# Remainder tiles behind the kv products, and two kv products in one: a fused attention and MLP kernel on one core

## The chip, the core and the metric

The kernel runs on one core of a Trainium2 chip. A core has a matrix engine (PE, with its weight loader PEld), a vector engine (DVE), a scalar engine (ACT), GpSimd (POOL) and a queue engine (SP); each works through its own instructions in order and waits for the others by semaphores. Transfers are issued from SP, ACT or POOL and are carried out by 16 DMA engines. The metric is the device time of one execution in microseconds (us). The kernel before was timed six times: median 290.68 us, from 290.37 to 290.84.

## The reference

Eight batches of eight heads, 576 positions, head size 64. For each batch and head, `kv = kᵀ v` (64x64), `out = q kv`, and `out` is divided by its root mean square over the head's 64 elements and multiplied by `g_norm`. The heads side by side make rows `x` of 512. Then comes an MLP with a layer norm ahead of it and a residual:

```python
xn = (x - mean(x)) / sqrt(var(x) + 1e-6) * g_ln
out = x + relu(xn @ w_ch1) @ w_ch2        # 512 -> 2048 -> 512
```

Inputs and output are float32; the kernel multiplies in bfloat16.

## The kernel before, in words

**Tiles.** A batch has 576 rows: four *main tiles* of 128 rows and 64 rows left over. The leftovers of two batches (0 and 1, 2 and 3, and so on) make one *remainder tile* (`rem_tile`, named by the odd batch: 1, 3, 5, 7); the four remainder tiles form a ninth block that goes through the MLP last. A text such as "tile (3,2)" means main tile 2 of batch 3.

**Stages of a batch.** POOL loads k, v and q with a cast to bfloat16 (`load`, L92 to L94: two transfers per tensor). `kv_of` (L239) makes kv of all heads with 40 small matmuls, each with a 128x64 piece of k as weights; two heads stand side by side in the two column halves of the PE array, and two ACT copies put the result into `kv_pack`. `turn_q_dma` (L201) copies q on DVE into another order (L203), and SP transposes it by DMA (L205) into `qts[b]`. A tile (`Tile`, L258) then runs `o` (q times kv on PE: four matmuls for a main tile; eight for a remainder tile, which writes the two batches' 64 rows from the two column halves of the array, as `kv_of` does), `sq` (square, ACT), `red` (sum over the head, DVE), `root` (ACT), `y`, `x`, `xc` (three passes on DVE, L303, L322, L332), `var` (ACT) and `turn` (a DMA transpose of 128x512 on SP, L352, or in the first batches four PE transposes) into `xT_blk`, from which the MLP reads. The two PSUM buffers of `o` are freed by `y`.

**MLP.** `mm1` (L403) multiplies a block's `xT_blk` with w1, with ACT's Relu into `m1`; `mm2` (L450) multiplies `m1` with w2 and ends each tile with `finish` (L432): one DVE pass (L434) and two stores issued on SP (L447, L448).

**Order.** Everything is emitted by hand, in slots. `mm1` and `mm2` call `tick()` once for each unit of work (mostly four matmuls of 512 columns), and `tick` first emits what `at(slot, fn)` put into the agenda for that slot, sorted by the slot's fraction. Block b has `mm1` in slots 32b to 32b+15 and `mm2` in 32b+16 to 32b+31; batch 2's `mm1` runs in two halves of two tiles each (slots 64 to 71 and 72 to 79). So a step of the agenda lands on PE between two units of an earlier block's MLP, and on DVE, ACT, SP and POOL at the matching place of their queues. `plan_tile(s, make, turn_at, on_pe)` (L371) puts `o`, `sq`, `red` at s, `y`, `x`, `xc` at s+2, `var` at s+6 and the turn at `turn_at`. The loop at L633 plans the loads, `kv_of`, `turn_q_dma` and tiles of batches 3 to 7, and the remainder tiles 3, 5 and 7; L630 plans remainder tile 1.

**Loads.** `load_batch` (L96) first makes POOL copy one element of a transposed tile to a one-element buffer `gate`: POOL's queue waits there until that transpose has landed, and the batch's six transfers stand behind. Batch b uses buffers b % 2. For batch 4 a second such copy reads the last element of batch 2's block, which is tile (2,3)'s turned rows.

Of the kernel before, what the change touches and what calls it, by code (L numbers as in the profile page):

```python
# [14 lines left out]
def kernel(  # L15
# [11 lines left out]
    nc = tc.nc  # L27
    f32 = mybir.dt.float32
# [5 lines left out]
    B, H, S, D = q.shape  # L34
# [3 lines left out]
    nK = Dm // 128  # L38
    nDe = Dh // 128
    HP = H // 2  # L40
# [3 lines left out]
    J, JJ, JP = 4, 5, 9  # L44
    S_LO = 64 * JJ
    EPS = 1e-6
    NB = 2
# [8 lines left out]
    ps_m = ctx.enter_context(tc.psum_pool(name="ps_m", bufs=1))  # L56
# [15 lines left out]
    q_in = [consts.tile([128, H, JJ, D], bf16, name=f"q_in{i}") for i in range(NB)]  # L72
    k_in = [consts.tile([128, H, JJ, D], bf16, name=f"k_in{i}") for i in range(NB)]
    v_in = [consts.tile([128, H, JJ, D], bf16, name=f"v_in{i}") for i in range(NB)]
    kv_g = consts.tile([128, HP, 128], bf16)
    kv_pack = [consts.tile([128, HP, 128], bf16, name=f"kv_pack{i}") for i in range(4)]
# [9 lines left out]
    def lo(t, b, h0=0, h1=H):  # L86
        return t[b, h0:h1, :S_LO, :].rearrange("h (p j) d -> p h j d", j=JJ)

    def up(t, b, h0=0, h1=H):
        return t[b, h0:h1, S_LO:, :].rearrange("h (p j) d -> p h j d", j=J)  # L90

    def load(dst, t, b, h0=0, h1=H):  # L92
        nc.gpsimd.dma_start(dst[:64, h0:h1], lo(t, b, h0, h1))
        nc.gpsimd.dma_start(dst[64:, h0:h1, :J], up(t, b, h0, h1))  # L94

    def load_batch(b, *after):  # L96
        for element in after:
            nc.gpsimd.tensor_copy(gate, element)  # L98
        load(k_in[b % NB], k, b)
        load(v_in[b % NB], v, b)  # L100
        load(q_in[b % NB], q, b)

    def load_w1(c):
        n = Dh // 4
# [60 lines left out]
    qts, held, blks, rstds, m1s, q_ps = {}, {}, {}, {}, {}, {}  # L165
# [35 lines left out]
    def turn_q_dma(b):  # L201
        q_p = kv_in.tile([128, JJ, H, D], bf16, tag="qp", bufs=2)
        nc.vector.tensor_copy(q_p.rearrange("p j h d -> p h j d"), q_in[b % NB])  # L203
        q_t = qt_pool.tile([128, JJ, HP, 128], bf16, tag="qt", name="qt")
        nc.sync.dma_start_transpose(  # L205
            q_t.rearrange("p j hp t -> p (j hp) t"), q_p.rearrange("p j h d -> p (j h d)"))
        qts[b] = q_t
# [28 lines left out]
            nc.vector.tensor_mul(kv_g[D:, self.hps, D:], self.odd[D:], g[D:])  # L236
            del self.even, self.odd

    def kv_of(b):  # L239
        kv_ps = ps_m.tile([128, HP, D], f32, tag="misc", name="kv_ps")  # L240
        kvp = held[b] = kv_pack[b % 4]
        for hp in range(HP):
            for j in range(JJ):
                for hh in range(2):
                    h = 2 * hp + hh
                    nc.tensor.matmul(kv_ps[hh * D:hh * D + D, hp, :],  # L246
                                     lhsT=k_in[b % NB][:, h, j, :], rhs=v_in[b % NB][:, h, j, :],
                                     start=(j == 0), stop=(j == JJ - 1))
        nc.scalar.copy(kvp[:D, :, :D], kv_ps[:D])  # L249
        nc.scalar.copy(kvp[D:, :, D:], kv_ps[D:])  # L250

    def new_block(n, bufs):
        x_blk = xpool.tile([128, 4, Dm], f32, tag=f"x{n}", bufs=bufs, name="x_blk")
        st_blk = xpool.tile([128, 3, 4], f32, tag=f"st{n}", bufs=bufs, name="st_blk")
        xT_blk = xpool.tile([128, nK, 512], bf16, tag=f"xT{n}", bufs=bufs, name="xT_blk")
        return x_blk, st_blk, xT_blk
# [98 lines left out]
    def main_tile(b, j, pool=None, tag="ops"):  # L355
        q_t, kvp = qts[b], held[b]
        if b not in blks:
            blks[b] = new_block("main", 3)
        return Tile([(slice(0, 128), lambda hp: q_t[:, j, hp, :], kvp)], blks[b], j, pool, tag)

    def rem_tile(b):
        mms = []
        for half, bb in enumerate((b - 1, b)):
            qt, kp = qts.pop(bb), held.pop(bb)
            mms.append((slice(half * 64, (half + 1) * 64),
                        lambda hp, qt=qt: qt[:, J, hp, :64], kp))
        if "rem" not in blks:
            blks["rem"] = new_block("rem", 1)
        return Tile(mms, blks["rem"], b // 2)

    def plan_tile(s, make, turn_at, on_pe):  # L371
        box = []

        def first():
            t = make()
            box.append(t)
            t.o()
            t.sq()
            t.red()

        def second():
            t = box[0]
            t.y()
            t.x()
            t.xc()

        def third():
            box[0].var()

        def fourth():  # L390
            box[0].turn(on_pe)

        at(s, first)
        at(s + 2, second)
        at(s + 6, third)
        at(turn_at, fourth)

    def m1_of(b):
# [20 lines left out]
    def rstd_of(b):  # L419
        rstd = work.tile([128, 4], f32, tag="rstd", bufs=3, name="rstd")  # L420
        nc.scalar.activation(rstd, blks[b][1][:, 2, :], func=AF.Sqrt, scale=1.0 / Dm, bias=eps_sb)  # L421
        nc.vector.reciprocal(rstd, rstd)  # L422
        rstds[b] = rstd
# [45 lines left out]
    def at(slot, fn):  # L469
        agenda.setdefault(int(slot), []).append((slot, fn))  # L470
# [119 lines left out]
    def next_loads():  # L590
        nc.gpsimd.memset(k_in[0][64:, :, J], 0.0)
        nc.gpsimd.memset(v_in[0][64:, :, J], 0.0)
        load_batch(2)

    at(1, before_1)
    at(2, before_2)
    at(5, lambda: t[2].turn(True))
    at(5.1, before_5)
    at(9.5, next_loads)
    at(11, lambda: t[3].turn(True))  # L600
    for i in range(4):
# [17 lines left out]
    at(14.5, q_start)  # L619
    at(19, q_turns)  # L620
    at(22, lambda: kv_of(1))
    for j, s, tn in ((0, 24, 30), (1, 27, 34), (2, 31, 38), (3, 35, 42)):
        plan_tile(s, lambda j=j: main_tile(1, j), tn, True)
    at(46, lambda: rstd_of(1))

    at(36, lambda: kv_of(2))
    at(36.9, lambda: turn_q_dma(2))
    for j, s, tn in ((0, 45, 51), (1, 49, 55), (2, 53, 61), (3, 57.5, 64)):
        plan_tile(s, lambda j=j: main_tile(2, j), tn, False)
    plan_tile(62, lambda: rem_tile(1), 69, False)  # L630
    at(78, lambda: rstd_of(2))

    for b in range(3, B):  # L633
        s = 32 * b
        at(47 if b == 3 else s - 60,
           lambda b=b: load_batch(b, qts[b - 1][:1, J, HP - 1, 127:],
                                  *([blks[2][2][:1, nK - 1, 511:]] if b == 4 else [])))
        d = -41 if b == 3 else -45
        at(s + d + (1 if b < 5 else 0), lambda b=b: kv_of(b))
        at(s + d + 1.7, lambda b=b: turn_q_dma(b))  # L640
        for j in range(J):
            o = s + d + (11 if b == 3 else 13) + 5 * j
            plan_tile(o, lambda b=b, j=j: main_tile(b, j), o + 6, False)
        if b % 2:
            plan_tile(s - 14, lambda b=b: rem_tile(b), s - 8, False)
        at(s + 14, lambda b=b: rstd_of(b))
    at(32 * B + 14, lambda: rstd_of("rem"))


# [56 lines left out]
```

## Time and profile before

| | |
|---|---|
| median of six runs | 290.68 us |
| the profiled execution's own time | 290.74 us |
| its span in the profile | 288.9 us |
| PE busy | 281.9 us, 98% of the span |
| ACT, DVE, POOL busy | 153.3, 149.9, 40.9 us |
| bytes moved | 36.76 MB, mean 127 GB/s |

The span runs from the first to the last instruction; the execution's own time has 1.8 us more around it. PE's ends are modelled and its matmuls overlap, so its busy share hides gaps of some tenths of a microsecond: the starts of neighbouring groups of matmuls are what can be relied on. In the timeline a row is a group of equal instructions, with its start, its length, the engine (SPq is SP's queue, with the issue time of a transfer), the line, the operation, and in brackets the idle time before it with what ended it. Times are from the span's start.

### The profile page before, as it was taken

How to read it: one execution, taken by the hardware profiler on the slowest of the kernel's cores; microseconds unless marked ns; L12 is line 12 of the kernel's file. 1: busy time of each engine (PE TensorE's matmuls, PEld its weight loads, DVE VectorE, ACT ScalarE, POOL GpSimd, SP SyncE). 2: the span in 40 equal slices, each digit the busy share in tenths (PEclk: the TensorE clock that was granted, in tenths of full speed). 3: DMA queues.
4: the chain of work that ended last, by engine and by line, in shares of the span. 5: the costliest groups of instructions: out<-in, count | busy, mean ns of one | idle time of the engine just before them, and what ended most of it. 6: DMA issues, size and time to landing. Idle time of an engine off the chain costs nothing.

```text
span 288.9 us, 5753 instructions
## 1 busy us (share of the span) xinstructions
PE 281.9 (98%) x2295; PEld 158.1 (55%) x2295; DVE 149.9 (52%) x331; ACT 153.3 (53%) x333; POOL 40.9 (14%) x69
## 2 busy tenths in 40 slices
PE   8999999999999999999999999999999999999994
PEld 3579746995479644444444444444444444444444
DVE  5774119838897783764376935762578200220022
ACT  3577844985379733872288318921893066016400
POOL 8522510050005004100500032000000000000000
PEclk9999999999999999999999999999999999999999
DMA  7999999979886959996994189947203410230033
GB/s 217 198 208 203 198 189 197 215 117 187 134 173 103 194 106 158 202 158 120 159 217 68 39 152 218 155 84 152 54 18 64 102 36 0 47 82 19 0 73 75
DMA packets 67546, 36.76 MB, mean 127 GB/s; under 512 B 35516, under 2 KB 62524, under 8 KB 67520
## 3 DMA queue, kind: packets, MB, share of 16 engines
q0 software_dynamic: 28528, 17.76, 43.7%
q1 hardware_dynamic: 38480, 17.91, 31.0%
q10 hardware_dynamic: 512, 0.72, 0.7%
q8 instruction: 18, 0.29, 0.4%
q14 instruction: 8, 0.07, 0.1%
HBM read 36.71 MB, written 9.44 MB: 160 GB/s over the span
## 4 chain that ended last, share of the span: by engine, by line
PE 83%; DMA 14%; SPq 1%; issue 1%; POOL 0%; DVE 0%; POOLq 0%
PE p L429 40%; PE p L413 39%; DMA w_sb<-in_moe_w_ch_dram 11%; PE o_ps L271 3%; DMA v_in<-in_v_dram 2%; PE kv_ps L246 2%; DMA xT_blk<-xc 1%; SPq L205 1%; PE tp L348 0%; POOL w_sb L106 0%; DVE o_sb L434 0%; POOLq L690 0%
## 5 line engine op out<-in xcount | busy, mean ns | idle before, releaser
L413 PE MATMUL p<-xT_blk,w_sb 128*128 128x128 bf16 (+2 forms) x1024 | 131.6, 286 | 0.7 <-DMA xT_blk<-xc 0.3
L429 PE MATMUL p<-w_sb,m 128*128 128x512 bf16 (+2 forms) x608 | 129.1, 368 | 0.1
L416 ACT ACTIVATE m<-p 128x512 bf16<-128x512 f32 x144 | 85.3, 595 | 43.1 <-PE p L413 40.6
L413 PEld LDWEIGHTS <-w_sb 128*128 128x128 bf16 x1024 | 78.6, 98 | 45.0 <-issue 1.5
L429 PEld LDWEIGHTS <-m 128*128 128x128 bf16 x608 | 57.0, 98 | 62.2 <-issue 0.2
L434 DVE SCALAR_TENSOR_TENSOR o_sb<-p,rstd,x_blk 128x512 f32<-128x512 f32 (+2 forms) x38 | 27.3, 720 | 52.2 <-PE p L429 46.6
L277 ACT ACTIVATE sq<-o_ps 128x512 f32<-128x512 f32 x35 | 20.9, 596 | 42.2 <-PE o_ps L271 42.2
L298 DVE TENSOR_REDUCE ss<-sq 128x8 f32<-128x512 f32 x35 | 23.7, 678 | 13.2 <-ACT sq L277 13.1
L340 ACT ACTIVATE dev<-x_blk,st_blk 128x512 f32<-128x512 f32 x36 | 25.7, 714 | 6.2 <-DVE st_blk L326 6.1
L332 DVE SCALAR_TENSOR_TENSOR xc<-x_blk,st_blk,g_ln_sb 128x512 bf16<-128x512 f32 x34 | 25.6, 752 | 1.2
L303 DVE TENSOR_TENSOR y<-o_ps,inv 128x512 f32<-128x512 f32 x33 | 22.8, 692 | 3.4 <-PE p L413 0.5
L322 DVE SCALAR_TENSOR_TENSOR x_blk<-y,g_norm_sb 128x512 f32<-128x512 f32 x33 | 22.8, 691 | 1.1
L315 DVE RECIPROCAL inv<-rms 128x8 f32<-128x8 f32 x36 | 7.2, 201 | 23.2 <-ACT rms L308 23.2
L422 DVE RECIPROCAL rstd<-rstd 128x4 f32<-128x4 f32 x9 | 1.6, 175 | 31.3 <-ACT rstd L421 31.1
L308 ACT ACTIVATE rms<-ss,eps_sb 128x8 f32<-128x8 f32 x36 | 10.7, 296 | 11.1 <-DVE ss L298 10.9
L98 POOL COPY gate<-qt 1x1 bf16<-1x1 bf16 x5 | 0.9, 176 | 106.6 <-DMA qt<-q_p 106.6
L271 PEld LDWEIGHTS <-qt 128*128 128x128 bf16 (+1 forms) x156 | 10.2, 100 | 8.2 <-issue 1.7
L271 PE MATMUL o_ps<-kv_pack,qt 128*128 128x128 bf16 (+1 forms) x156 | 13.7, 220 | 0.2
L198 PE MATMUL p<-fill_sb 128*128 128x512 bf16 x27 | 8.9, 485 | 1.2 <-DVE eps_sb L137 1.2
L340 ACT ACTIVATION_READ_ACCUMULATOR dev<-x_blk,st_blk 128x1 f32 x36 | 6.8, 189 | 0.0
L249 ACT CAST kv_pack<-kv_ps 64x256 bf16<-64x256 f32 x7 | 2.6, 366 | 7.8 <-PE kv_ps L246 7.8
L246 PEld LDWEIGHTS <-k_in 128*64 128x64 bf16 x280 | 5.0, 112 | 2.7 <-issue 2.6
(80 smaller groups left out, 110.8 us busy)
## 6 DMA issues: line engine op xcount, KB each, us to landing
out_dram<-o_sb SPq DMA_DIRECT2D x70, 128.0 KB, 2.5
w_sb<-in_moe_w_ch_dram POOLq DMA_DIRECT2D x8, 512.0 KB, 15.4
q_in<-in_q_dram POOLq DMA_DIRECT2D x7, 320.0 KB, 12.4
k_in<-in_k_dram POOLq DMA_DIRECT2D x7, 320.0 KB, 5.7
v_in<-in_v_dram POOLq DMA_DIRECT2D x7, 320.0 KB, 8.6
q_in<-in_q_dram POOLq DMA_DIRECT2D x8, 256.0 KB, 12.4
k_in<-in_k_dram POOLq DMA_DIRECT2D x7, 256.0 KB, 6.9
v_in<-in_v_dram POOLq DMA_DIRECT2D x7, 256.0 KB, 10.8
```

The lines of the kernel that those rows point to most:

```text
L246: nc.tensor.matmul(kv_ps[hh * D:hh * D + D, hp, :], lhsT=k_in[b % NB][:, h, j, :], rhs=v_in[b % NB][:, h, j, :], start=(j == 0), stop=(j = ...
L271: nc.tensor.matmul(flat[rows, hp * 128:(hp + 1) * 128], lhsT=lhsT_of(hp), rhs=kvp[:, hp, :], start=True, stop=True)
L277: nc.scalar.activation(self.sq_t, self.o_ps, func=AF.Square)
L298: nc.vector.tensor_reduce(self.ss, self.sq_t, axis=AX.X, op=ALU.add)
L303: nc.vector.tensor_mul(self.y_t, self.o_ps, self.inv().to_broadcast([128, H, D]))
L322: nc.vector.scalar_tensor_tensor(x_blk[:, ts].rearrange("p (h d) -> p h d", h=H), in0=self.y_t, scalar=1.0, in1=g_norm_sb.to_broadcast([12 ...
L332: nc.vector.scalar_tensor_tensor(self.xc_t, in0=x_blk[:, self.ts], scalar=st[:, 1, self.ts:self.ts + 1], in1=g_ln_sb, op0=ALU.add, op1=ALU ...
L340: nc.scalar.activation(dev, x_blk[:, ts], func=AF.Square, bias=st[:, 1, ts:ts + 1], accum_out=st[:, 2, ts:ts + 1])
L413: nc.tensor.matmul(p1[:, i, :], lhsT=w1_sb[:, kk, de * 128:(de + 1) * 128], rhs=blk[2][:, kk, sl], start=(kk == 0), stop=(kk == nK - 1))
L416: nc.scalar.activation(m1[:, de0:de0 + per, sl], p1, func=AF.Relu)
L429: nc.tensor.matmul(p2[:, c0:c1], lhsT=m1s[b][:, de, ts * 128:(ts + 1) * 128], rhs=w2_sb[:, de, c0:c1], start=(de == 0), stop=(de == nDe - 1))
L434: nc.vector.scalar_tensor_tensor(o_sb[:, c0:c1], in0=p2[:, c0:c1], scalar=rstds[b][:, ts:ts + 1], in1=blks[b][0][:, ts, c0:c1], op0=ALU.mu ...
```

## The change

Written as slots of the agenda, rounded down as `at` does:

| step | before | after |
|---|---|---|
| kv of batch 3, remainder tile 1 | 56, 62 (its `y` 64) | 56, directly behind it (its `y` 64) |
| tiles (3,0) to (3,3) | 66, 71, 76, 81 | 67, 71, 75, 79 |
| their turns | 72, 77, 82, 87 | 73, 77, 81, 85 |
| remainder tile 3, kv of batch 4 | 82, 84 | kv 85, the tile directly behind it (`y` 88) |
| q of batch 4 to SP | 84 | 86 (behind tile (3,3)'s turn) |
| tiles of batch 4 | 96, 101, 106, 111 | 97, 101, 106, 111 |
| remainder tile 5, kv of 6, kv of 7 | 146, 147, 179 | 152: kv of 6 and 7 in one PSUM tile, the tile directly behind (`y` 154) |
| turns of remainder tiles 1, 3, 5 | 69, 88, 152 | 69, 94, 160 |
| loads at slot 132 | k, v, q of 6 | q of 6, k and v of 6, k and v of 7 |
| loads at slot 164 | k, v, q of 7 | q of 7 |

`kv_of(*bs)` makes one PSUM tile for all its batches, all matmuls first, then the copies. The matmuls of each batch and tile, their shapes and their number are those of before. The core of the diff:

```diff
-    def load_batch(b, *after):
+    def load_batches(what, *after):
         for element in after:
             nc.gpsimd.tensor_copy(gate, element)
-        load(k_in[b % NB], k, b)
-        load(v_in[b % NB], v, b)
-        load(q_in[b % NB], q, b)
+        tensors = {"k": (k_in, k), "v": (v_in, v), "q": (q_in, q)}
+        for name, b in what:
+            dst, src = tensors[name]
+            load(dst[b % NB], src, b)
...
-    def kv_of(b):
-        kv_ps = ps_m.tile([128, HP, D], f32, tag="misc", name="kv_ps")
+    def kv_of(*bs):
+        kv_ps = ps_m.tile([128, len(bs), HP, D], f32, tag="misc", name="kv_ps")
...
-    plan_tile(62, lambda: rem_tile(1), 69, False)
...
-    for b in range(3, B):
-        s = 32 * b
-        at(47 if b == 3 else s - 60,
-           lambda b=b: load_batch(b, qts[b - 1][:1, J, HP - 1, 127:],
-                                  *([blks[2][2][:1, nK - 1, 511:]] if b == 4 else [])))
-        d = -41 if b == 3 else -45
-        at(s + d + (1 if b < 5 else 0), lambda b=b: kv_of(b))
-        at(s + d + 1.7, lambda b=b: turn_q_dma(b))
+    at(47, lambda: load_batches((("k", 3), ("v", 3), ("q", 3)), turned_q(2)))
+    at(68, lambda: load_batches((("k", 4), ("v", 4), ("q", 4)),
+                                turned_q(3), blks[2][2][:1, nK - 1, 511:]))
+    at(100, lambda: load_batches((("k", 5), ("v", 5), ("q", 5)), turned_q(4)))
+    at(132, lambda: load_batches((("q", 6), ("k", 6), ("v", 6), ("k", 7), ("v", 7)),
+                                 turned_q(5)))
+    at(164, lambda: load_batches((("q", 7),), turned_q(6)))
+    at(115, lambda: kv_of(5))
+    for s, bs, rem, x_at, tn in ((56, (3,), 1, 64, 69), (85, (4,), 3, 88, 94),
+                                 (152, (6, 7), 5, 154, 160)):
+        at(s, lambda bs=bs: kv_of(*bs))
+        plan_tile(s + .1, lambda rem=rem: rem_tile(rem), tn, False, x_at)
+    plan_tile(210, lambda: rem_tile(7), 216, False)
+    for b, at_q, at_o, step in ((3, 56.7, 67, 4.3), (4, 86, 97, 4.75),
+                                *((b, 32 * b - 43.3, 32 * b - 32, 5) for b in range(5, B))):
+        at(at_q, lambda b=b: turn_q_dma(b))
         for j in range(J):
-            o = s + d + (11 if b == 3 else 13) + 5 * j
+            o = at_o + step * j
             plan_tile(o, lambda b=b, j=j: main_tile(b, j), o + 6, False)
-        if b % 2:
-            plan_tile(s - 14, lambda b=b: rem_tile(b), s - 8, False)
```

## The prediction

> **What bounds the kernel now.** I read the page's busy rows first, then the list of waits on PE, then the timeline at the places that the change touches.
>
> ```profile
> PE 281.9 (98%) x2295; PEld 158.1 (55%) x2295; DVE 149.9 (52%) x331; ACT 153.3 (53%) x333; POOL 40.9 (14%) x69
> PE p L198 <- DVE eps_sb L137: 1.2, 1, 1.2
> PE p L413 <- DMA xT_blk<-xc: 0.3, 1, 0.3
> ```
>
> PE is busy for 98%, and the list of waits (engine, line, what it waited for: us, times, longest) puts 0.3 us on the stretch that the change touches. So no work can be hidden better; time can only come from gaps between matmuls that the busy share covers up. The timeline shows them as distances of starts. First PE and its weight loader around remainder tile 5 and the kv of batch 6:
>
> ```profile
> 156.22 1.89 PE L429 MATMUL p<-w_sb,m 128*128 128x512 bf16 x8
> 158.04 0.41 PE L271 MATMUL o_ps<-kv_pack,qt 128*64 128x128 bf16 x8
> 158.39 1.04 PE L429 MATMUL p<-w_sb,m 128*128 128x512 bf16 x4
> 159.35 0.82 PE L246 MATMUL kv_ps<-v_in,k_in 128*64 128x64 bf16 x40
> 160.11 2.12 PE L429 MATMUL p<-w_sb,m 128*128 128x512 bf16 x9
> 159.35 0.71 PEld L246 LDWEIGHTS <-k_in 128*64 128x64 bf16 x40 [0.42 <-issue]
> ```
>
> Eight matmuls of 512 columns take (1.89-0.38)/7 = 0.216 us each, so 1.73; the next group starts after 1.82: 0.09 lost on the way into the 128*64 form, where the weight loader too stands idle (0.42). The remainder tile holds PE for 0.09+0.35 = 0.44 us, of which its matmuls need 8 x (0.41-0.219)/7 = 0.22 (0.219 is the length of one). The kv: 159.35 is 0.96 behind 158.39 where four matmuls need 0.86, so 0.10 in, then 0.76: 0.85 us, of which 40 x (0.82-0.196)/39 = 0.64 is work. Each excursion into the 128*64 form thus costs 0.21 to 0.22 us besides its work.
>
> Second, the start of batch 3's `mm1`:
>
> ```profile
> 106.57 3.11 SPq L205 DMA_TRANSPOSE qt<-q_p  x1
> 109.73 1.27 SPq L352 DMA_TRANSPOSE xT_blk<-xc  x1
> 111.69 0.40 PE L271 MATMUL o_ps<-kv_pack,qt 128*128 128x128 bf16 x4
> 112.36 1.89 PE L413 MATMUL p<-xT_blk,w_sb 128*128 128x512 bf16 x8 [0.27 <-DMA xT_blk<-xc]
> ```
>
> Tile (3,3)'s turn stands on SP behind q of batch 4, issues at 109.73 and lands about 112.3. Tile (4,0) starts 0.30 us late (0.517 behind the last L429 start instead of 0.216; it waits for q's transpose), and L413 follows 0.67 later instead of four matmuls at 0.056 = 0.22: 0.45. Together 0.75 us lost. A smaller one: (3,0) at 83.14 waits 0.2 us for q of batch 3.
>
> Third, the half-block before, at slot 72:
>
> ```profile
> 76.15 0.75 DVE L434 SCALAR_TENSOR_TENSOR o_sb<-p,rstd,x_blk 128x512 f32<-128x512 f32 x1
> 76.81 0.82 DVE L203 COPY q_p<-q_in 128x2560 bf16<-128x2560 bf16 x1
> 81.22 0.75 DVE L434 SCALAR_TENSOR_TENSOR o_sb<-p,rstd,x_blk 128x512 f32<-128x512 f32 x1
> 81.88 0.68 DVE L298 TENSOR_REDUCE ss<-sq 128x8 f32<-128x512 f32 x1
> 81.99 0.47 SPq L447 DMA_DIRECT2D out_dram<-o_sb  x1
> 85.75 5.16 SPq L352 DMA_TRANSPOSE xT_blk<-xc  x3
> 87.97 2.24 PE L413 MATMUL p<-xT_blk,w_sb 128*128 128x256 bf16 x19
> 88.44 0.18 POOL L98 COPY gate<-xT_blk 1x1 bf16<-1x1 bf16 x1 [5.05 <-DMA xT_blk<-xc]
> ```
>
> Slot 72 is the ninth matmul of the row at 87.97: 87.97+8x0.109 = 88.84. It needs tile (2,3)'s turn, the first of the three L352 at 85.75; POOL's gate waits for the same one and starts at 88.44, so it landed about 88.39: 0.45 us to spare.
>
> **What the Trainium skill says.** "TensorEngine Tiling (Array Packing)", Tiling Modes, Key Properties: "Mode switching requires drain: Changing tiling mode (not just tile) drains the TensorE". The 0.21 us per excursion agree with that; kv and remainder tiles have the same 128*64 form, so no switch should lie between them. "TensorE: Matmul & The Clock Gate", Back-to-back issue gap: N/2.4+2.5 ns, 215.8 for 512 columns; the trace has 0.216. The same page, Architectural detail, calls ACT and DVE strict FIFO: what is put earlier in DVE's order delays all behind it. "DMA: Bandwidth & Descriptors", Issuing engines are not separate DMA queues: transfers of all queues interleave on the same 16 DMA engines; here a turn takes 2.4 us to land at the least, 3.9 at the median, 8.7 at most.
>
> **The change part by part.**
>
> *Merges.* Kv 3 with remainder 1, kv 4 with remainder 3, and kv 6, kv 7 and remainder 5 are seven excursions before, three after: four fewer. At a joint the first pair may restart (kv's first pair took 49 ns against 28 later, the remainder tile's 77 against 53), so I take 0.03 us off 0.22: 0.19 per merge; bounds 0 (a joint drains like a switch) and 0.22. The ACT copies of kv 6 and 7 are 4 x 0.37 us at slot 152, with no tile of theirs before slot 160.
>
> *Remainder 1 at slot 56.* Its `red` (L298) moves on DVE from 81.88 to behind the L434 at 76.15, ahead of the L203 copy. It fills 0.68-0.08 = 0.60 us there. Queued behind: the copy, (2,3)'s `red`, `y`, `x`, `xc`, and the L434 of 81.22, all 0.60 later; the second L434 (82.47) is not, since the `red` no longer stands before it. Who waits: SP. Its q transpose was held by two stores until 78.08 and moves only to about 78.3. But the store at 81.99 follows the L434 at once and moves to 82.59, and from there SP issues without a break through 85.75, so (2,3)'s turn issues at 86.34 and lands about 88.98. PE gets to slot 72 earlier: by 0.19 (merge) and by 0.2 (tile (3,0), a slot later, finds q of 3 landed at 83.3, its start being 83.6), at 88.45. It starts near 89.05: a new wait of 0.6 us, and PE stands 0.21 behind the old timeline. This merge's gain and the 0.2 are swallowed here. `o` of (2,3) now reuses the PSUM buffer that `y` of (2,2) frees at 74.52; PE comes at 74.73: nothing, narrowly.
>
> *Loads of batch 4* go 0.6 later with the gate. The last v piece lands 99.87+0.6 = 100.5; kv 4 at slot 85 comes at about 100.9 (slot 84 was 100.27; +0.86 for a slot, -0.45 without remainder 3 ahead, +0.21). 0.4 to spare, as before: nothing. q lands 102.95+0.6; DVE comes to the copy after remainder 3's `red`, about 103.6.
>
> *Batch 3 closer, q of 4 behind (3,3)'s turn.* (3,3) starts two slots earlier and its turn comes ahead of q on SP, at about 103.7; even with 7 us to land it is there before 111.4. The q transpose follows at 105.0 (3.11 to issue, 5.0 to land): 110.1, and (4,0) needs it at 112.3 (slot 97). Both waits go: -0.75.
>
> *Loads of batch 7's k and v at slot 132.* The gate falls about 0.75 earlier than 138.57, the first piece issues near 138.3 and lands 5.7 later, 144.0 (k_in of before: 5.7). Nine more follow. Pieces of one batch landed 1.64 us apart from 94.8 on, 1.92 from 144.8, 2.13 from 176.4 and 2.39 from 118.8, where more stores and turns ran beside them. Five at 1.92 and four at 1.65 to 2.13 end at 160.2 to 162.1. Kv 7 starts near 163.1 (kv 6 stood at 159.35 in slot 147; five slots are 4.3; less 0.45 for remainder 5, less 0.75, plus 0.64 of kv 6). Cover 1.0 to 2.9 us: nothing. Turns of batch 5 land slower beside it, but (5,3) comes to SP near 165 and its block starts at 171.
>
> *Sum.* +0.21 at slot 72, -0.75 at slot 96, -0.19 (kv 4) and -0.38 (kv 6, 7, remainder 5): -1.11 us. 290.74 becomes 289.63; against the median, 290.68, 289.57. I say 289.6.
>
> **Rivals.**
> 1. *The joints drain too*: kv to remainder tile costs a full switch. For it: no two such groups adjoin in this trace. Then -0.54 remains: 290.15.
> 2. *No new wait at slot 72*, if SP makes up the 0.6: against it, SP has no idle time between 81.99 and 85.75. Then -1.7: 288.97.
> 3. *A load is late by tenths*: kv 4 (0.4 to spare) or kv 7 waits 0.4 to 0.8 us: 290.0 to 290.4.
> 4. *Slower: v of batch 7.* At 2.12 us per piece kv 7 begins to wait; at 2.25 the gain is gone; above 2.31, 291.3 and more. 2.39 was seen once, under six stores and three turns; here the stores fall on the first pieces alone.
>
> **How the numbers follow.** Chances: forecast 0.62 (own range 289.3 to 289.8), rival 1 0.10, rival 2 0.08, rival 3 0.13, rival 4 0.07. A measurement of this kernel tells 0.2% (0.58 us) from no change, so faster means below 290.10: forecast, rival 2 and some of rivals 1 and 3, 0.79; same 0.14; slower 0.07. The range leaves out half of rival 2 and rival 4, with the far end of rival 3: 289.0 to 290.35.
>
> **What would show it.** Right: no wait on qt or xT near slot 96; L271 in the 128*64 form directly behind L246 three times, without the loader's 0.42 between; a wait of about 0.6 us of L413 for a turn near 88.5; L205 of q 4 behind an L352. Wrong: kv_ps waiting for v_in near 101 or 163, or a 0.2 us distance at a joint.

## The result, and the profile after

The changed kernel takes 292.88 us (median of 16 runs, 290.98 to 293.85) against 290.53 us for the kernel before (median of 36): ratio 1.0064, 95% interval 1.005 to 1.0077. It is 0.6% slower, where the prediction had 289.6. Its times fall into two groups, six of 17 executions (the profiled one included) at 291.0 to 291.4 us and eleven at 292.8 to 293.9 (medians 291.2 and 293.1); they differ in the matrix engine's clock, which the eleven show at 0.991 to 0.994 in the mean and the six at 0.998 to 1.0. The profiled execution took 292.94 us, 2.20 more than that of before, and is one of the eleven. Behind the diff the lines are numbered three higher: L413 is now L416, L429 L432, L271 L274, L352 L355, L434 L437; L246 is L247, L205 L206, L203 L204.

The page of the changed kernel: busy row, clock in 40 slices of the span, and the instruction queue's row (packets, MB, share of the DMA engines).

```profile
PE 282.2 (97%) x2295; PEld 158.9 (55%) x2295; DVE 150.0 (52%) x331; ACT 153.2 (53%) x333; POOL 40.9 (14%) x69
PEclk9999999999998999999999999999999999999999
q8 instruction: 18, 0.29, 0.4%
```

PE's work is the same. The 13th slice of the clock row (87.3 to 94.6 us) is below full speed; in the kernel before all 40 are 9. The last row, which I passed over, will be the cause; it is the same in the kernel before:

```profile
PEclk9999999999999999999999999999999999999999
q8 instruction: 18, 0.29, 0.4%
```

The list of waits on PE has one new entry:

```profile
PE p L416 <- DMA xT_blk<-xc: 2.3, 1, 2.3
```

It is the wait of slot 72, which the prediction put at 0.6 us. In stretches of the same execution (busy us and number of instructions by engine, then granted clock, DMA share, GB/s):

```profile
88.00:91.70 3.70, 1.45 (x14) 1.05 (x13) 1.97 (x5) 1.03 (x2) 0.18 (x1) 1.00 0.68 79
91.70:95.10 3.40, 3.40 (x20) 2.40 (x18) 1.67 (x5) 2.13 (x6) 3.19 (x5) 0.50 0.56 65
95.10:98.00 2.90, 2.90 (x30) 2.62 (x28) 1.52 (x3) 2.51 (x5) 0.90 (x2) 1.00 1.39 194
```

One microsecond after PE has gone on, its clock is halved for 3.4 us: 1.7 us lost besides the wait. The timeline has the chain up to it, and the merges further on:

```profile
73.34 0.39 PE L274 MATMUL o_ps<-kv_pack,qt 128*64 128x128 bf16 x8
76.65 0.68 DVE L301 TENSOR_REDUCE ss<-sq 128x8 f32<-128x512 f32 x1
77.25 0.82 DVE L204 COPY q_p<-q_in 128x2560 bf16<-128x2560 bf16 x1
82.42 0.47 SPq L450 DMA_DIRECT2D out_dram<-o_sb  x1
86.20 10.99 SPq L355 DMA_TRANSPOSE xT_blk<-xc  x4
87.37 1.04 PE L416 MATMUL p<-xT_blk,w_sb 128*128 128x256 bf16 x8
90.66 4.36 PE L416 MATMUL p<-xT_blk,w_sb 128*128 128x256 bf16 x24 [2.25 <-DMA xT_blk<-xc]
90.73 0.18 POOL L98 COPY gate<-xT_blk 1x1 bf16<-1x1 bf16 x1 [7.36 <-DMA xT_blk<-xc]
...
104.17 0.82 PE L247 MATMUL kv_ps<-v_in,k_in 128*64 128x64 bf16 x40
104.83 0.39 PE L274 MATMUL o_ps<-kv_pack,qt 128*64 128x128 bf16 x8
106.93 1.30 SPq L355 DMA_TRANSPOSE xT_blk<-xc  x1
108.34 3.13 SPq L206 DMA_TRANSPOSE qt<-q_p  x1
114.66 1.03 PE L416 MATMUL p<-xT_blk,w_sb 128*128 128x512 bf16 x4
115.53 0.39 PE L274 MATMUL o_ps<-kv_pack,qt 128*128 128x128 bf16 x4
165.75 1.46 PE L247 MATMUL kv_ps<-v_in,k_in 128*64 128x64 bf16 x80
167.03 0.39 PE L274 MATMUL o_ps<-kv_pack,qt 128*64 128x128 bf16 x8
```

DVE's order is the predicted one, and tile (2,3)'s turn issues at 86.20 (86.34 in the prediction). It lands at 90.6 (PE at 90.66 and POOL's gate at 90.73 both go on with it) instead of 88.98: 4.4 us after its issue, not 2.64. All the rest is as worked out: tile rows of 128*64 directly behind the kv rows, and near 114.66 no wait any more.

Where the time lies shows best in stages, cut at the first matmul of a part of the MLP (the end is PE's last). In us, from the profiled execution of each kernel; the experiments are those of the next section:

| stage | before | after | remainder 3 alone moved | remainder 1 at 62, batch 3 old | remainder 1 at 62 | late sum (run 7) |
|---|---|---|---|---|---|---|
| start to `mm1` of batch 2 (slot 64) | 81.19 | 80.81 | 80.95 | 81.04 | 81.38 | 80.70 |
| to `mm2` of batch 3 (slot 112) | 45.65 | 48.56 | 44.67 | 44.69 | 44.47 | 44.47 |
| to `mm2` of batch 4 | 29.38 | 29.38 | 29.38 | 29.38 | 29.38 | 29.38 |
| to `mm2` of batch 6 | 59.21 | 58.75 | 59.21 | 58.76 | 58.76 | 58.76 |
| to the end | 69.76 | 69.76 | 69.76 | 69.76 | 69.76 | 69.76 |

The first row varies by some tenths with the opening's loads, whatever the kernel (with remainder 1 at 62, for one, kv of batch 1 waits 0.32 us for v at 39.03). The loss is in one stage: +2.91, which is 2.25 of wait and 1.7 of half clock, and leaves 1.04 gained; the late sum, which has no wait there, gains 1.18. Kv 6 and 7 with remainder tile 5 gain 0.46.

**The cause.** The trace lists every DMA packet. Those of queue 8 have 16 KB each, and there are 18 for PE's 2295 matmuls and 2295 weight loads: one for 4590/18 = 255 instructions. The Trainium skill, "Runtime: NRT & Kernel Launch", Instruction fetch mechanics, has the same: blocks of 16 KiB, 256 instructions, fetched by a DMA queue of the engine's own while it runs, at a cost it calls "mostly hidden". It was hidden from PE, not from the neighbours. A turn is 512 packets of 256 bytes and then 32 of 4 bytes, and without a fetch beside turn (2,3) PE or POOL goes on 0.4 to 0.5 us behind the last of these ("by" is when they had ended):

```
turn (2,3)        issued   fetch runs       of the 32 last packets   last one   PE or POOL goes on
before            85.75    89.03 - 90.00    32 by 87.94              87.94      88.44
after             86.20    88.40 - 89.36    30 by 88.34, 2 later     89.54      90.66
```

In the kernel before the fetch comes 0.6 us after this turn has landed. It does hit something, remainder tile 1's turn, issued at 87.14: 30 of its 32 last packets have ended by 89.22, two end at 90.18, and it lands at 91.1. Nobody waits for that. In the changed kernel PE is earlier by the merge and the turn is later by DVE's order, and the same fetch falls on the turn that PE needs next: two packets are left when it begins, they start only when it has ended, and PE goes on 1.1 us behind them instead of 0.5. What happens inside the DMA engines, and why this last step is longer too, no run shows.

Turns elsewhere do the same. I take all profiles of this document, and the turns during which no load moved anything: 148 met no fetch between issue and landing and took 2.4 to 3.0 us; 20 met one that began 0.2 to 2.1 us behind their issue, and took 3.2 to 4.7. Fetches that began earlier or later than that gave both.

### The profile page after: what moved, and what is told of

Its sections match the earlier page's. It is cut to its first block, busy times and chain, and to the rows that moved or that the text cites. A ratio compares the mean times of both kernels' runs of the same rounds, so it can differ in the third digit from the quotient of the medians.

```text
span 291.0 us, 5755 instructions
## 1 busy us (share of the span) xinstructions
PE 282.2 (97%) x2295; PEld 158.9 (55%) x2295; DVE 150.0 (52%) x331; ACT 153.2 (53%) x333; POOL 40.9 (14%) x69
## 2 busy tenths in 40 slices
DMA packets 67546, 36.76 MB, mean 126 GB/s; under 512 B 35516, under 2 KB 62524, under 8 KB 67520
## 4 chain that ended last, share of the span: by engine, by line
PE 83%; DVE 7%; DMA 4%; ACT 2%; issue 1%; SPq 1%; DVEq 0%; POOLq 0%
PE p L416 40%; PE p L432 38%; DMA v_in<-in_v_dram 2%; PE o_ps L274 2%; DMA xT_blk<-xc 2%; PE kv_ps L247 2%; DVE ss L301 1%; DVE x_blk L325 1%; DVE y L306 1%; DVE o_sb L437 1%; ACT m L419 1%; ACT rms L311 1%; DVE x_blk L292 0%; DVE xc L550 0%; SPq L355 0%
## 5 line engine op out<-in xcount | busy, mean ns | idle before, releaser
L416 PE MATMUL p<-xT_blk,w_sb 128*128 128x128 bf16 (+2 forms) x1024 | 133.7, 288 | 2.7 <-DMA xT_blk<-xc 2.3
L432 PE MATMUL p<-w_sb,m 128*128 128x512 bf16 (+2 forms) x608 | 128.2, 368 | 0.0
L416 PEld LDWEIGHTS <-w_sb 128*128 128x128 bf16 x1024 | 79.1, 98 | 47.7 <-DMA xT_blk<-xc 2.5
L432 PEld LDWEIGHTS <-m 128*128 128x128 bf16 x608 | 57.3, 98 | 63.0
L437 DVE SCALAR_TENSOR_TENSOR o_sb<-p,rstd,x_blk 128x512 f32<-128x512 f32 (+2 forms) x38 | 27.2, 720 | 47.7 <-PE p L432 44.8
L274 PEld LDWEIGHTS <-qt 128*128 128x128 bf16 (+1 forms) x156 | 10.5, 102 | 6.1 <-issue 0.4
L274 PE MATMUL o_ps<-kv_pack,qt 128*128 128x128 bf16 (+1 forms) x156 | 13.7, 221 | 0.0
L199 PEld LDWEIGHTS <-fill_sb 128*128 128x128 bf16 x27 | 3.1, 122 | 5.5 <-issue 3.3
```

Of the source, the lines that this page charges most:

```text
L274: nc.tensor.matmul(flat[rows, hp * 128:(hp + 1) * 128], lhsT=lhsT_of(hp), rhs=kvp[:, hp, :], start=True, stop=True)
L416: nc.tensor.matmul(p1[:, i, :], lhsT=w1_sb[:, kk, de * 128:(de + 1) * 128], rhs=blk[2][:, kk, sl], start=(kk == 0), stop=(kk == nK - 1))
L432: nc.tensor.matmul(p2[:, c0:c1], lhsT=m1s[b][:, de, ts * 128:(ts + 1) * 128], rhs=w2_sb[:, de, c0:c1], start=(de == 0), stop=(de == nDe - 1))
L437: nc.vector.scalar_tensor_tensor(o_sb[:, c0:c1], in0=p2[:, c0:c1], scalar=rstds[b][:, ts:ts + 1], in1=blks[b][0][:, ts, c0:c1], op0=ALU.mu ...
```

## The experiments

Two theories. F: a fetch of PE's instructions while turn (2,3) is under way is what delays it; where fetch and turn are kept apart, the prediction's sum holds. G, the rival: the turn is late because of its new place in DVE's and SP's order, and the fetch is a bystander. A third question came up on the way: which edit removes the waits at slot 96. The fetch can be moved without touching the schedule, since it goes by PE's count of instructions: the opening fills (18 matmuls on zeros, L490) can be cut into more and narrower ones.

**1. The changed kernel, 40 PE instructions more ahead of everything.**

```diff
-    fill(18)
+    p1 = fill(12)
+    for _ in range(26):
+        nc.tensor.matmul(p1[:, :118], lhsT=fill_sb[:, :128], rhs=fill_sb[:, :118], ...)
```

> The changed kernel, with 6 of the 18 opening fill matmuls of 512 columns replaced by 26 of 118 columns: the same columns, 40 PE instructions more before everything else, so PE's instruction fetch (every 256 instructions, one packet of 16 KB on the queue named instruction) comes about 2 us earlier at slot 71 than 88.4. Theory F (the fetch's packet holds up the turn of tile (2,3) on its DMA engine): the fetch falls near 86.3, the turn issues near 86.2 and lands by 89.1, L416 waits 0.7 us at most, no half clock; 289.4 to 289.9. Theory G (the turn is slow there whatever PE fetches, because of stores and turns in a row): it lands at 90.5 as before, 291.1 or 293.

290.34 us (14 runs, 290.12 to 291.22; ratio 0.9995, interval 0.9987 to 1.0003): 2.5 us faster than the changed kernel, by other opening fills alone. The timeline of this kernel:

```profile
85.42 1.42 SPq L451 DMA_DIRECT2D out_dram<-o_sb  x1
86.88 3.98 SPq L355 DMA_TRANSPOSE xT_blk<-xc  x3
89.49 2.69 PE L416 MATMUL p<-xT_blk,w_sb 128*128 128x256 bf16 x23 [1.22 <-DMA xT_blk<-xc]
```

The fetch moved to 85.50, and the turn lands 2.6 us after its issue again. The time missed its expectation because the fetch, which ran to 86.47, now fell on SP's store: its issue took 1.42 us instead of 0.59, and the turn behind it left 0.68 later. (In the changed kernel too the issue on SP that the fetch met, that of the turn behind (2,3), took 2.17 us instead of 1.22.) The wait of 1.22 is 0.62 above the predicted one: 289.57 + 0.62 = 290.2.

**2. The kernel before, 12 instructions more** (two fills as eight of 128 columns), so that its fetch comes near the landing of the turn.

> The kernel before, with 2 of the 18 opening fills replaced by 8 of 128 columns: 12 PE instructions more, the same columns. Theory F: the fetch of 89.03 moves to about 88.35, onto the turn of tile (2,3), which landed at 88.39: it lands between 89.9 and 90.5, PE waits 1.1 to 1.6 us at slot 72; 291.6 to 292.2, or up to 294 in executions in which the clock halves. Theory G: as before, 290.5.

291.27 us (20 runs; ratio 1.0027, 1.0014 to 1.0039), in two groups of ten: 290.43 to 290.84, and 291.7 to 293.13. The profiled execution is of the first: its fetch stood at 88.17, 0.5 us behind the turn's last packet. So the kernel before, its schedule untouched, loses over a microsecond in half of its executions; the expectation held for that half alone, and none shows the half clock (mean clock 0.997 to 1.0). No execution of the slower half left a profile; the next experiment puts the fetch further onto the turn.

**5. The same with 20 instructions more** (four fills as 14 of 146 columns).

> The kernel before with 20 more PE instructions ahead of everything (4 of the 18 opening fills as 14 of 146 columns). Theory F (a fetch of PE instructions that falls on a turn under way delays it): the fetch stands about 87.9 us, turn (2,3), issued about 85.8, is under way in every execution and lands about 90.2; PE waits 1.0 to 1.6 us at slot 72, where the kernel before waits for nothing; 291.6 to 293 in all executions, no more in two groups. Theory G (only the changed order on DVE and SP makes the turn late): the order is that of before, so no wait, 290.5.

291.95 us (4 runs, 291.9 to 292.46; ratio 1.0054, 1.0041 to 1.0067), one group. Timeline:

```profile
85.52 5.32 SPq L352 DMA_TRANSPOSE xT_blk<-xc  x3
90.10 2.14 PE L413 MATMUL p<-xT_blk,w_sb 128*128 128x256 bf16 x18 [1.34 <-ACT dev L340]
90.17 0.18 POOL L98 COPY gate<-xT_blk 1x1 bf16<-1x1 bf16 x1 [7.02 <-DMA xT_blk<-xc]
```

The fetch ran from 86.91 to 88.41, a microsecond earlier than expected; 12 of the turn's 32 last packets had ended by 87.55, the other twenty ended at 89.17 to 89.22 (eleven of them had begun by 87.59), and it landed 4.6 us after its issue. (PE's bracket names an ACT instruction; POOL's gate at 90.17 shows that it was the turn.) The wait of 1.34 is the whole loss, 290.53 + 1.34 = 291.87, and here the clock stayed at full speed. DVE's and SP's order is that of before: G falls.

**3. The changed kernel with remainder tile 1 back at slot 62**, all else changed.

```diff
-    for s, bs, rem, x_at, tn in ((56, (3,), 1, 64, 69), (85, (4,), 3, 88, 94),
+    at(56, lambda: kv_of(3))
+    plan_tile(62, lambda: rem_tile(1), 69, False)
+    for s, bs, rem, x_at, tn in ((85, (4,), 3, 88, 94),
```

> The changed kernel with remainder tile 1 back at slot 62. Its reduction is again behind the q copy on DVE, so the turn of (2,3) issues near 85.6 and lands near 88.2; the merge at kv 3 is lost (0.19). Theory F: PE reaches slot 72 near 88.5, the fetch falls near 88.7, behind the landing: no wait; 289.2 to 289.8. Theory G (only the issue time counts): the turn lands 0.6 us earlier than at 90.56, PE waits 1.4 us; 290.5 or, with the half clock, 292.

289.13 us (5 runs, 289.0 to 289.51; ratio 0.9949, 0.9937 to 0.9961): faster than both kernels, and 0.07 below the range that F expected. No wait at slot 72, none near slot 96. PE passes slot 72 in its stride, with the turn issued 0.27 us earlier than in the changed kernel:

```profile
85.93 5.44 SPq L355 DMA_TRANSPOSE xT_blk<-xc  x3
87.94 3.66 PE L416 MATMUL p<-xT_blk,w_sb 128*128 128x256 bf16 x32
88.62 0.45 POOL L98 COPY gate<-xT_blk 1x1 bf16<-1x1 bf16 x1 [5.04 <-DMA xT_blk<-xc]
```

But the fetch stands at 88.37 here, 0.25 us behind the turn's last packet at 88.12: it is a near miss too, if one that held in all five runs.

**4. The changed kernel with ten fills at slot 72**, which keep PE busy during the wait. They add 20 instructions behind the fetch and no result that is read.

```diff
+    at(72, lambda: fill(10))
```

> The changed kernel with 10 matmuls of 512 columns on zeros (2.16 us of PE work that nobody reads) just ahead of slot 72, inside the wait of 2.25 us. They stand behind the fetch in PE's order and do not move it. If the half clock is due to PE's idle time: no half clock in any run, all runs near 291.1, the turn still landing near 90.5. If the clock falls for another reason: two groups of times again, up to 293.

291.27 us (8 runs, 291.17 to 291.73; ratio 1.0028, 1.0018 to 1.0038), one group, mean clock 0.997 to 1.0. Its timeline:

```profile
88.31 2.32 PE L199 MATMUL p<-fill_sb 128*128 128x512 bf16 x10
90.98 1.26 PE L416 MATMUL p<-xT_blk,w_sb 128*128 128x256 bf16 x10 [0.35 <-DMA xT_blk<-xc]
```

The turn lands as late as in the changed kernel (issued at 86.25, 4.7 us), but the slower of the two groups is gone. So the half clock comes of PE's standing still, and costs the median 1.6 us; the lateness accounts for the rest: 289.57 + 2.25 - 0.6 = 291.2.

**6. The changed kernel, with remainder tile 1's `red` emitted at slot 62**, where it was, so that DVE and SP keep the order of before up to slot 72, while its `o` stays behind kv 3.

```diff
-            t.red()
+            if red_at is None:
+                t.red()
...
+        if red_at is not None:                  # 62 for remainder tile 1
+            at(red_at, lambda: box[0].red())
```

> The changed kernel with remainder tile 1's sum (red) emitted at slot 62 again, so DVE and SP have the order of before up to slot 72, while the merge with kv 3 stays. Theory F: turn (2,3) issues about 85.7, the fetch (PE is still earlier by the merge) comes about 88.1 to 88.4, close to the landing: if it hits, the turn lands about 90 and PE waits about 1.5 us, 290.4, or 292 with the half clock; if it just misses, 288.9. Theory G: no wait, 288.8, in every execution.

290.67 us (11 runs; ratio 0.9999, 0.9981 to 1.0017), in three groups: four at 288.82 to 289.77, four at 290.55 to 290.75, three at 291.3 to 291.67. In the profiled execution (of the first) the turn's last packets ended at 87.75 and the fetch began at 87.95. With the two 0.2 us apart, the spread from execution to execution may decide; the other ten left no profile, so this is not shown. Some of the spread is another wait: in the profiled one kv of batch 4 stood 0.5 us for v. G expected 288.8 in each.

**7. The same, with 16 of the opening fills as 8 float32 matmuls**, meant to take 24 instructions away and so to put the fetch later.

> The same as the one with the late sum, and 24 PE instructions fewer ahead of everything (16 of the opening fills as 8 float32 matmuls of 256 columns), so that the fetch comes about 1 us later, near 89.2, behind the landing of turn (2,3). Theory F: no wait at slot 72, no half clock, one group of times, 288.7 to 289.1. Theory G: the same time as with the late sum alone.

289.92 us (22 runs, 288.78 to 291.15; ratio 0.9978, 0.9965 to 0.9991), as spread as the sixth. The lever failed: the trace shows two matmuls for each float32 one, and the fetch stood at 87.86. It says nothing for or against F and counts as a second sample of the sixth; its profiled execution is a clean one (the last column of the table).

**9, 10, 11. The fetch put behind the wait.** 244 instructions more in the opening are 12 short of a whole block, so the later fetches fall *later*. The same edit to the changed kernel, to the kernel before, and to the one with the late sum:

```diff
-    fill(18)
+    p1 = fill(2)
+    for _ in range(138):
+        nc.tensor.matmul(p1[:64, :59], lhsT=fill_sb[:, :64], rhs=fill_sb[:, :59], ...)
```

> The changed kernel as it is, with 244 more PE instructions in the opening (16 of the 18 fills as 138 of 59 columns): 12 short of a whole block of 256, so the fetches that follow come 12 instructions later and the one of 88.40 falls behind the first matmul of slot 72, which waits for turn (2,3) itself. Theory F: turn (2,3), issued about 86.2, lands about 88.9 as the prediction had it; the wait at slot 72 is about 0.6 us, no half clock, one group of times, 289.4 to 289.9. Theory G (the later place in SP's order makes the turn take 4.4 us): still a wait of about 2.2 us, and 291 to 293.9.

> The kernel before with the same opening. Its fetch at 89.03 was already behind the landing of turn (2,3), so theory F and theory G both expect 290.5 within 0.3. It shows whether the changed opening costs or gains anything by itself.

> The changed kernel with the late sum of remainder tile 1 and the same opening, so that the fetch falls behind the first matmul of slot 72. Theory F: turn (2,3) lands about 88.2 in every execution, no wait at slot 72, the spread of 288.8 to 291.7 of the late sum alone shrinks to one group at 288.6 to 289.1. Theory G: times as spread as with the late sum alone, median 290 to 290.7.

The absolute times miss, and those of the changed kernel are not one group: the opening is not free. The kernel before itself goes from 290.69 to 294.1 us with it (6 runs, 292.46 to 294.72; ratio 1.0114), with the clock below full speed in the second and third slice of its page, ahead of everything that was changed:

```profile
PEclk9779999999999999999999999999999999999999
```

Behind the opening the stages can still be compared, in one profiled execution each. From slot 64 to slot 112 the control takes 45.64 us (45.65 with the old opening), the changed kernel 45.00 (48.56 with the old opening) and the late sum 44.47. The times agree with that. The changed kernel takes 292.55 us (12 runs, 290.46 to 293.69; ratio 1.0058, 1.0042 to 1.0075), 1.55 less than the control; the late sum takes 292.05 (5 runs, 291.32 to 292.18; 1.0044, 1.0031 to 1.0057), 2.05 less. Among executions of one mean clock (0.991 to 0.994), the medians are 293.69 (control, 3), 292.55 (changed, 8) and 292.05 (late sum, 5): -1.14 and -1.64, where the prediction's sum is -1.11 and its rival without a new wait -1.7. That the first agrees to 0.03 is in part luck: the control has three such executions, and the wait was not the 0.6 of the sum. The timeline of the changed kernel with this opening (all of it about 3.9 us later):

```profile
90.14 5.35 SPq L355 DMA_TRANSPOSE xT_blk<-xc  x3
92.71 2.46 PE L416 MATMUL p<-xT_blk,w_sb 128*128 128x256 bf16 x21 [0.35 <-DMA xT_blk<-xc]
92.79 0.65 POOL L98 COPY gate<-xT_blk 1x1 bf16<-1x1 bf16 x1 [5.47 <-DMA xT_blk<-xc]
```

The turn lands 2.6 us after its issue and PE waits 0.35 us; the fetch comes at 93.76. With the schedule of the changed kernel untouched and only the fetch elsewhere, the change gains about what the sum said, and G is out. Against the schedule the fetch moved by 1.4 us; twelve instructions were worth 0.86 in the second experiment, and the wait of 0.35 lies between. The rest is no more than what the fetch moves between profiles of one order of instructions (89.03 in the kernel before, 88.21 in the twelfth experiment).

**8. The third experiment, and batch 3's tiles (66, every 5 slots), q of 4 (84) and batch 4's first tiles (96, every 5) at the slots of before.**

```diff
-    for b, at_q, at_o, step in ((3, 56.7, 67, 4.3), (4, 86, 97, 4.75),
+    for b, at_q, at_o, step in ((3, 56.7, 66, 5), (4, 84.7, 96, 5),
```

> The changed kernel with remainder tile 1 at slot 62 as in the third experiment, and besides batch 3's tiles, q of batch 4 and batch 4's tiles at the slots of before. By the sum of the prediction the 0.75 us at slot 96 come back and nothing else: 289.13 + 0.75 = 289.9, with the wait of the first mm1 of batch 3 for turn (3,3) and of tile (4,0) for q in the list of waits. A rival, that the closer tiles gain nothing by themselves: 289.1.

289.57 us (20 runs, 289.26 to 291.09; ratio 0.9968, 0.9959 to 0.9977). In the median 0.44 slower than the third, but not 0.75, and *no wait at slot 96*:

```profile
101.52 9.67 PE L432 MATMUL p<-w_sb,m 128*128 128x512 bf16 x44
111.03 0.39 PE L274 MATMUL o_ps<-kv_pack,qt 128*128 128x128 bf16 x4
111.25 4.48 PE L416 MATMUL p<-xT_blk,w_sb 128*128 128x512 bf16 x20
```

44 matmuls at 0.216 are 9.5 us, and tile (4,0) follows after 9.51. The second stage is 44.69, 0.22 above that of the third: the 0.2 of tile (3,0), which again waits for q of 3. The rest of the 0.44 lies outside this stage and is not explained (the two runs are from different chips, with 290.53 and 290.5 us for the kernel before). The prediction's step was wrong: the closer tiles don't clear slot 96. That called for one more.

**12. The kernel before, with remainder tile 3 alone moved** (kv 4 at 85 with the tile behind it, `y` at 88, turn at 94).

> The kernel before with one part of the change alone: kv of batch 4 at slot 85 with remainder tile 3 right behind it, its second step at 88 and its turn at 94. Batch 3's tiles, q of batch 4, remainder tiles 1 and 5 and the loads of batch 7 stand as before. The prediction's step credits the 0.75 us at slot 96 to batch 3's closer tiles and to q of batch 4 behind turn (3,3), so it expects only the merge here: 290.5 - 0.19 = 290.3, with the waits at slot 96 still there. The rival from the run with batch 3 as before, that remainder 3's later second step lets q of batch 4 pass on DVE about 2.4 us earlier and so clears both waits by itself: 290.5 - 0.94 = 289.6, L206 on SP near 104.4 and no wait of L274 or L416 near slot 96. The fetch stays behind the landing of turn (2,3), as nothing ahead of slot 82 changes.

289.66 us (5 runs, 289.54 to 289.85) against 290.68: ratio 0.9966, 0.9952 to 0.9979. One edit of five gives 1.02 us; its second stage is 0.98 shorter. The kernel before on DVE shows why, in rows of its timeline that I had not looked at:

```profile
103.37 0.69 DVE L303 TENSOR_TENSOR y<-o_ps,inv 128x512 f32<-128x512 f32 x1
105.02 0.75 DVE L332 SCALAR_TENSOR_TENSOR xc<-x_blk,st_blk,g_ln_sb 128x512 bf16<-128x512 f32 x1
105.68 0.82 DVE L203 COPY q_p<-q_in 128x2560 bf16<-128x2560 bf16 x1
```

And the kernel of this run:

```profile
103.16 0.83 DVE L204 COPY q_p<-q_in 128x2560 bf16<-128x2560 bf16 x1 [0.56 <-issue]
104.09 3.42 SPq L206 DMA_TRANSPOSE qt<-q_p  x1
107.57 1.26 SPq L355 DMA_TRANSPOSE xT_blk<-xc  x1
110.91 0.39 PE L274 MATMUL o_ps<-kv_pack,qt 128*128 128x128 bf16 x4
```

In the kernel before the passes `y` to `xc` of remainder tile 3 stand on DVE ahead of the copy of q: the load of q has landed at 102.95, and DVE copies it only at 105.68. With the tile's second step at slot 88 the copy is there at 103.16, 2.5 us earlier; q and, behind it, turn (3,3) issue 2.5 and 2.2 us earlier on SP, and both waits are gone with SP's order unchanged.

**The best version** is that of the third experiment at 289.13 us: everything but the merge of remainder tile 1, with five runs behind it and the fetch 0.25 us away from the turn. The late sum shows 288.8 in its good executions and can't hold it.

## Why the prediction was wrong, step by step

**The step that failed** is "(2,3)'s turn issues at 86.34 and lands about 88.98 ... a new wait of 0.6 us". The issue held (86.20); the landing took 4.4 us instead of 2.64, because PE's instruction fetch at 88.40 fell on the turn's last packets. I took the latency from the same turn in the kernel before, and did not ask which other transfers of the DMA engines lay next to it: that one ended 0.6 us ahead of a fetch, and the sum put it 0.6 us later with PE 0.4 earlier. The term is 2.25, not 0.6.

**A step that was missing:** the half clock. The prediction priced a wait at its length. This one halved the clock too: 3.4 us at 0.50 cost 1.7 in the profiled execution, and ten of the other 16 show the same by their mean clock. Both together: 289.63 + 1.65 + 1.7 = 293.0 for the profiled execution (292.94), and 289.57 + 1.65 = 291.2 for the faster group (291.0 to 291.4).

**Slot 96:** right in size, wrong in its reason. The two waits went, worth 0.98 with the merge of kv 4 (0.94 in the sum); but moving remainder tile 3 does it alone (twelfth run), by DVE's rows because its second step comes later, and not the closer tiles. I had used that step only for the later DVE time of the copy, "about 103.6", and had not compared that with the 105.68 of before. What the closer tiles give is 0.22, the wait of tile (3,0), as the sum had it.

**Merges:** held. From kv to tile 29 ns pass between starts, like from pair to pair; rival 1 (the joints drain) is out. Kv 6, 7 and remainder 5 gained 0.46 (0.38 in the sum; the 0.03 that I had deducted for each joint isn't lost). In the times this third merge stays unproven: ratio 0.9968 with it (eighth run) and 0.9966 without (twelfth), intervals of 0.002 to 0.003; only the stage shows it.

**Rivals 3 and 4:** kv 7 never waited for v. Kv 4 did wait 0.5 us for v in the profiled execution of the sixth run, and its second stage is 45.06 us, 0.59 more than the seventh's:

```profile
100.62 0.82 PE L247 MATMUL kv_ps<-v_in,k_in 128*64 128x64 bf16 x40 [0.52 <-DMA v_in<-in_v_dram]
```

So its 0.4 to spare was as thin as it looked. No other profile shows this wait; in the changed kernel the late slot 72 puts kv 4 at 104.17.

**Rival 2** (no new wait, 288.97) is what the third run comes near, at the price of one merge, and what the sixth and seventh show at their best.

## What to carry to other kernels

Before a turn or load is made tight, put PE's instruction fetches on the same time axis: here one came every 255 or so PE instructions, it moved with the matmuls added ahead of it, and a turn that should have ended just in time beside one took about 2 us longer. A wait on PE is to be priced at its length, and again for the clock that may follow it. And when a wait goes, test each edit alone: here one of five did it all.

## What the runs showed that I had not expected

- A fetch of 16 KB takes 0.9 to 2.1 us; turn (2,3), where a fetch met its last packets, landed 4.4 to 4.7 us after its issue instead of 2.5 to 2.65, and a store's issue on SP took 1.42 instead of 0.59 us.
- Moving the fetch by 12 PE instructions in an opening of zeros changed an untouched schedule by over 1 us in ten of 20 executions.
- A wait of 2.25 us on PE halved its clock for 3.41 us, and eleven of 17 executions have the mean clock of that; waits of 1.2 and 1.34 us did not in the runs profiled. The Trainium skill, "TensorE: Matmul & The Clock Gate", What's actually happening, gives a free-running window of 3413 ns, which agrees with the length seen, and an idle window of about 3.4 us as what it takes; here less was enough.
- A row with 0.4% of the DMA time, 18 packets of 67546, decided between 289 and 293 us.
